# A fused attention and MLP kernel: dummy matmuls in longer pieces, and the list of steps in another order

## The chip, the cores and the metric

The kernel runs on one core of a Trainium2 chip. Its time is the device time of one execution in microseconds (us), taken as the median of several runs. The engines have their own instruction streams and run them strictly in order: TensorE (PE) for matrix products, VectorE (DVE) and ScalarE (ACT) for elementwise work, GpSimd (POOL) and SyncE (SP), which here mostly issue DMAs.

## The reference

Eight sequences ("images" in the step names, b = 0 to 7) with eight heads of 576 queries and 64 features. Each head has 16 beacon keys and values ahead of its own, and the mask is causal on the rest. The result, 4608 tokens of 512, goes through two matrix products with an ELU between them.

```python
scores = scale * np.matmul(q, k_all.transpose(0, 1, 3, 2))     # k_all = beacon_k, k
scores = np.where(causal, -1000000000.0, scores)
a = np.exp(scores - scores.max(-1, keepdims=True))
a /= a.sum(-1, keepdims=True) + 1e-09
x = np.matmul(a, v_all)        # v_all = beacon_v, v
...                            # heads side by side: x is 4608 x 512
h = x @ w_in                   # 512 x 2048
g = np.where(h > 0.0, h, np.exp(np.minimum(h, 0.0)) - 1.0)
return g @ w_out               # 2048 x 512
```

## The kernel before

The kernel is a set of small step functions and one long list of words. A word such as `F.3.10` calls the step `F` with the arguments 3 and 10. Every step issues its instructions in program order on the engines that it uses, so the list alone sets the order on each engine; across engines, semaphores hold an instruction until its operands are there and its buffer is free. There is no planner at run time: if an instruction has to wait, everything behind it on its engine waits too.

The steps that matter here:

- `warm.n` (L205) and `wm.n` (L212) are dummy matmuls on zeros, n of 512 columns or n of 128. They keep PE streaming in the opening, and nobody reads their result.
- `lq`, `lv`, `wi`, `wo` load queries and keys, values and weights. For images 0 to 2 `T` (L265) transposes queries and keys on PE, and `cq`, `ck` (L278) copy them out of PSUM on ACT or DVE.
- For images 3 to 7 `lk.b.0` and `lk.b.1` (L801) bring the queries and the keys of image b as bf16 into a scratch in device memory by POOL's queue; `lt.b.x` (L808) transposes one half of the heads of both out of that scratch, on SP's queue, into a buffer qst or kst (named by the half of the heads, two sets of buffers in turn); `lp.b.x` (L818) is a POOL copy of the beacon columns into the same buffer. The scores of a half need both loads and that half's own `lt` and `lp`.
- `S` (L319) are pieces of scores, `x` (L334) their exponentials on ACT, `m` (L339) the causal masks on DVE, `L` (L377) row sums, `W` (L377) the products with the values, `n` the reciprocal of the row sums by logarithm and exponential on ACT (L441, L444), `M` the scaling of the values' products on DVE.
- `F.t.i` (L518) is one piece of the first product for token tile t (512 tokens), `e` its exponential (L528), `u` its relu on ACT (L534) or, written `.v`, on DVE (L536), `k` (L548) the ELU put together on DVE. `r` and `g` (L555, L560) do the relu and the sum on DVE in another form, without `u`.
- `Q.t.a.b` (L625) are the matmuls a to b of the second product for tile t, in a scheme of seven half-size products instead of eight; `Z` builds sums of tiles for it on DVE (L573) or, written `.d`, by an accumulating DMA that POOL issues (L571). `J` (L642, L649) copies results out of PSUM and stores or accumulates them; some of those accumulations are POOL's (L656).
- For tiles 6 to 9 the first product is done by seven products too: `H`, `X`, `P` (L732), `K`, `E`, `U`, `V`.

POOL's DMAs take eight semaphore lanes in turn, DMASW0 to DMASW7: each of them waits for the landing of the one eight DMAs before it.

Of the kernel before, what the change touches and what calls it, by code (L numbers as in the profile page):

```python
# [17 lines left out]
def kernel(  # L18
# [819 lines left out]
    cq.0.3.1 S.0.3.1 m.0.3.0 x.0.3.1 m.0.0.3 L.0.A T.1.0.0 lv.0.0.1 m.0.2.2 n.0.A cq.1.0.0
    T.1.1.0 warm.4 S.0.2.1 ck.1.1.0 W.0.A.0 m.0.1.3 wi.2 S.0.3.3 W.0.A.1 x.0.2.1 M.0.A.0 M.0.A.1
    x.0.3.3 lv.0.3.4 S.1.1 S.0.3.2 cb.1.1 x.1.1 wi.1 x.0.3.2 m.0.2.3 m.0.3.3 F.0.4 cb.1.2 S.1.4  # L840
    m.0.3.2 x.1.4 e.0.4 L.0.B n.0.B W.0.B.0 S.1.3 x.1.3 F.0.3 r.0.4 g.0.4 cb.1.3 e.0.3 F.0.2
    M.0.B.0 S.1.0 u.0.2.v r.0.3 W.0.B.1 g.0.3 x.1.0 e.0.2 lq.1.0.4.8 T.1.2.0 M.0.B.1 F.0.5
    ck.1.2.0 u.0.5 T.1.3.0 k.0.2 S.1.6 m.1.0.0 F.1.5 e.0.5 cq.1.3.0 lq.2.0.0.4 x.1.6 S.1.2 H.1.1
    S.1.10 H.1.2 e.1.5 u.1.5.v k.0.5 F.1.2 u.1.2.v wi.0 x.1.10 F.1.4 x.1.2 e.1.2 k.1.5 S.1.5
    x.1.5 T.2.0.0 wi.3 u.1.4.v e.1.4 F.0.1 S.1.12 cq.2.0.0 F.0.0 u.0.1 T.2.1.0 x.1.12 e.0.1
    k.1.2 S.1.7 k.1.4 cq.2.1.0 e.0.0 F.1.0 x.1.7 S.1.11 u.0.0.v e.1.0 S.1.9 u.1.0.v lq.2.0.4.8
    F.0.6 x.1.11 S.1.8 x.1.9 k.1.0 x.1.8 F.1.6 u.0.6.v m.1.0.1 T.2.3.0 cb.2.3 e.0.6 T.2.2.0
    ck.2.3.0 m.1.1.1 ck.2.2.0 k.0.0 lv.1.0.1 m.1.1.0 F.0.7 cb.2.2 u.0.7.v lv.1.2.3.4 S.2.10
    x.2.10 wo.1 k.0.6 e.0.7 L.1.1 e.1.6 L.1.0 n.1.1 k.0.1 wo.0 n.1.0 u.1.6.v k.1.6 F.1.3 wo.2
# [136 lines left out]
```

## Time and profile before

| | before |
|---|---|
| median of 3 runs | 326.86 us (325.18 to 329.2) |
| the profiled execution's own time | 326.78 us |
| its span | 325.1 us |
| PE busy | 316.2 us (97%) |
| DVE busy | 294.0 us (90%) |
| ACT busy | 289.5 us (89%) |
| POOL busy | 122.0 us (38%) |
| granted PE clock, mean | 0.999 |

The span runs from the first busy instruction to the last; the 1.7 us between it and the execution's own time lie around it. Busy shares are means over the whole span, so the views by stretch of time, which the prediction shows, are needed beside them.

### The profile page before, as it was taken

The numbers are of one execution on the slowest core, as the hardware profiler recorded it, in microseconds if no ns is written. First come the engines' busy times: TensorE is split into PE (matmuls) and PEld (weight loads), VectorE is DVE, ScalarE is ACT, GpSimd is POOL, SyncE is SP. The second block draws the span as 40 slices with busy tenths as digits, with TensorE's granted clock in tenths as the row PEclk, the third lists the DMA queues.
The fourth block names the chain that finished last, engine by engine and source line by source line (L and its number), as shares of the span: only waits on it lengthen the run. The fifth ranks groups of instructions, "written<-read, shape, count | busy, mean of one in ns | idle before, by whom it ended". The sixth has DMA issues, their size and how long they took to land.

```text
span 325.1 us, 9115 instructions
## 1 busy us (share of the span) xinstructions
PE 316.2 (97%) x3743; PEld 226.4 (70%) x3744; DVE 294.0 (90%) x539; ACT 289.5 (89%) x479; POOL 122.0 (38%) x133
## 2 busy tenths in 40 slices
PE   8979999999999999999999999999999999999995
PEld 5647776656555655666555568788888888888884
DVE  2766998999989999989999999999999999998992
ACT  1988999998899999999999998999999999989910
POOL 8865693349318200527047085110401130041200
PEclk9999999999999999999999999999999999999999
DMA  9999999999999995599999997923293364476353
GB/s 112 167 183 202 190 193 183 155 156 168 158 172 165 187 103 105 78 175 149 175 141 153 179 78 104 124 68 98 35 162 67 66 96 68 100 87 123 89 93 129
DMA packets 141658, 42.53 MB, mean 131 GB/s; under 512 B 113201, under 2 KB 141617, under 8 KB 141617
## 3 DMA queue, kind: packets, MB, share of 16 engines
q0 software_dynamic: 106976, 26.35, 89.6%
q1 hardware_dynamic: 33920, 15.34, 23.4%
q8 instruction: 29, 0.48, 0.6%
q10 hardware_dynamic: 720, 0.26, 0.3%
q14 instruction: 13, 0.10, 0.1%
HBM read 37.22 MB, written 20.05 MB: 176 GB/s over the span
## 4 chain that ended last, share of the span: by engine, by line
PE 86%; ACT 6%; DVE 3%; DMA 2%; issue 1%; POOL 1%; DVEq 0%; POOLq 0%
PE ops L625 32%; PE hps L518 19%; PE hps L732 11%; PE sc L319 7%; PE ut L377 6%; PE sa L732 4%; ACT et L334 4%; PE sx L625 2%; PE lt L377 2%; DMA kst<-in_k_dram 2%; ACT e L528 1%; PE lt L426 1%; DVE hi L278 1%; ACT hi L278 1%; POOL qst L136 0%
## 5 line engine op out<-in xcount | busy, mean ns | idle before, releaser
L334 ACT ACTIVATE et<-sc 128x1024 f16<-128x1024 f32 (+2 forms) x114 | 104.8, 973 | 5.2 <-PE sc L319 5.0
L625 PEld LDWEIGHTS <-gt 128*128 128x128 f16 x864 | 83.2, 98 | 17.6 <-issue 1.2
L518 PE MATMUL hps<-xT,w_in 128*128 128x512 f16 (+1 forms) x384 | 79.7, 344 | 0.1
L656 POOL DMA_DIRECT2D out_dram<-osb x18 | 22.6, 1256 | 112.0 <-ACT osb L649 71.7
L625 PE MATMUL ops<-w_out,gt 128*128 128x256 f16 x416 | 55.0, 273 | 0.0
L625 PE MATMUL ops<-wt,gt 128*128 128x256 f16 x400 | 53.4, 273 | 0.0
L518 PEld LDWEIGHTS <-w_in 128*128 128x128 f16 x384 | 34.4, 98 | 27.0 <-issue 4.9
L548 DVE SCALAR_TENSOR_TENSOR gt<-e,r 128x512 f16<-128x512 f32 x74 | 49.5, 683 | 0.7 <-ACT r L534 0.4
L528 ACT ACTIVATE e<-hps 128x512 f32<-128x512 f32 x80 | 47.8, 617 | 2.4 <-PE hps L518 1.8
L149 POOL DMA_DIRECT2D v<-in_v_dram x40 | 38.2, 1226 | 17.2 <-issue 6.5
L777 DVE SCALAR_TENSOR_TENSOR gt<-e,r 128x512 f16<-128x512 f32 x64 | 42.7, 683 | 1.3 <-ACT e L760 0.5
L534 ACT ACTIVATE r<-hps 128x512 f16<-128x512 f32 x48 | 29.5, 622 | 0.3 <-DVE gt L548 0.3
L339 DVE TENSOR_TENSOR et<-et,triu 128x1024 f16<-128x1024 f16 (+5 forms) x66 | 27.0, 448 | 1.7 <-ACT et L334 1.7
L732 PEld LDWEIGHTS <-w_in 128*128 128x128 f16 x256 | 24.6, 98 | 4.2 <-issue 0.4
L760 ACT ACTIVATE e<-qst 128x512 f32<-128x512 f32 x40 | 25.8, 648 | 1.5 <-DVE qst L749 1.4
L573 DVE TENSOR_TENSOR gt<-gt 128x2048 f16<-128x2048 f16 (+1 forms) x24 | 25.8, 1083 | 0.0
L377 PEld LDWEIGHTS <-v 128*32 128x32 f16 (+1 forms) x800 | 17.4, 96 | 10.4 <-issue 3.0
L571 POOL DMA_DIRECT2D gt<-gt x6 | 9.7, 1619 | 35.8 <-DVE s L573 28.9
L749 DVE TENSOR_TENSOR qst<-hps,kst 128x512 f32<-128x512 f32 x32 | 21.5, 683 | 0.1
L536 DVE TENSOR_SCALAR r<-hps 128x512 f16<-128x512 f32 x26 | 17.9, 687 | 4.1 <-ACT e L528 2.7
L377 PE MATMUL ut<-et,v 128*32 128x464 f16 (+3 forms) x560 | 20.9, 296 | 0.0
L400 DVE TENSOR_TENSOR qkp<-qkp,et 128x1344 f16<-128x1344 f16 (+2 forms) x33 | 19.3, 585 | 0.5
(134 smaller groups left out, 561.8 us busy)
## 6 DMA issues: line engine op xcount, KB each, us to landing
out_dram<-sm SPq DMA_DIRECT2D x18, 256.0 KB, 2.4
out_dram<-osb POOLq DMA_DIRECT2D x18, 256.0 KB, 4.6
out_dram<-osb SPq DMA_DIRECT2D x17, 256.0 KB, 5.1
v<-in_v_dram POOLq DMA_DIRECT2D x24, 128.0 KB, 7.7
gt<-gt POOLq DMA_DIRECT2D x6, 512.0 KB, 7.1
scr<-in_q_dram POOLq DMA_DIRECT2D x5, 576.0 KB, 15.1
scr<-in_k_dram POOLq DMA_DIRECT2D x5, 576.0 KB, 16.2
w_in<-in_moe_w_in_dram POOLq DMA_DIRECT2D x8, 256.0 KB, 8.7
```

The lines of the kernel that those rows point to most:

```text
L149: nc.gpsimd.dma_start(out=vt[b][r0:r0 + n, j, :, :], in_=v[b, :, ilo[j]:ilo[j] + n, :].rearrange("h s d -> s h d"),)
L334: nc.scalar.activation(out=ets[b, d][:, :, a - EC2 * d:e - EC2 * d], in_=sc[b, g][:, :, a - c0:e - c0], func=AFT.Exp, bias=0.0, scale=SCALE)
L339: nc.vector.tensor_tensor(out=o, in0=o, in1=i, op=ALU.mult)
L377: nc.tensor.matmul(out=t[32 * i:32 * (i + 1), a - qa:e - qa], lhsT=ones[0:kc[j], :] if half is None else v16[0:kc[j], j, h, half:D:2], rhs ...
L518: nc.tensor.matmul(out=h[:, n_, :], lhsT=w_in16[:, cc, P * fc:P * (fc + 1)], rhs=xt[k][:, cc, a - TT * k:e - TT * k], start=(cc == 0), sto ...
L528: nc.scalar.activation(out=eb[t, i], in_=flat(hp[t, i]), func=AFT.Exp, bias=0.0, scale=1.0)
L534: nc.scalar.activation(out=rb[t, i], in_=flat(hp[t, i]), func=AFT.Relu, bias=0.0, scale=1.0)
L548: nc.vector.scalar_tensor_tensor(out=half(t, i), in0=eb[t, i], scalar=1.0, in1=rb[t, i], op0=ALU.subtract, op1=ALU.min)
L573: (nc.vector if eng == "v" else nc.gpsimd).tensor_tensor(out=o_, in0=a_, in1=b_, op=op_)
L625: nc.tensor.matmul(out=half_of(xy[t, n_], qd), lhsT=lw[:, P * qd:P * (qd + 1)], rhs=wt_[:, c, :], start=(first and c == 0 and (qd == 0 or ...
L732: nc.tensor.matmul(out=hx[t, g, n_][:, c, :], lhsT=lw, rhs=rh, start=(first and c == 0 and k_ == 0), stop=(k_ == 1), skip_group_check=True)
L777: eng.scalar_tensor_tensor(out=o_, in0=v_(eb[t, g, ph]), scalar=1.0, in1=v_(rb[t, g, ph]), op0=ALU.subtract, op1=ALU.min)
```

## The change

Only the list of words changes. In it, twelve `wm.4` (four dummy matmuls of 128 columns each) have become twelve `warm.1` (one of 512 columns). All other steps are there as before, with these exceptions in which engine does a piece: seven output copies net go from ACT to DVE, one copy of the first product's scheme and two relus of it from DVE to ACT, and among the plain relus three more are ACT's, two fewer DVE's, and one less takes the form `r`, `g`. The order of the words is another one from the first line on; in the opening PE's own order stays nearly what it was. The step functions are untouched, so their line numbers are the same in both.

The list has 1502 words in both; the first lines, and those around image 6's loads:

```diff
-    warm.4 wm.4 lq.0.0.0.4 wm.4 wm.4 wm.4 warm.4 lq.0.1.0.4 wm.4 ident bt bk wm.4 T.0.0.0 wm.4
-    cb.0.0 ck.0.0.0 cb.0.1 lq.0.0.4.8 T.0.1.0 S.0.0.0 T.0.0.1 cq.0.1.0 cq.0.0.1 S.0.1.0 x.0.0.0
...
+    warm.1 warm.1 warm.4 warm.1 warm.1 warm.1 warm.4 lq.0.0.0.4 lq.0.1.0.4 ident bt bk
+    lq.0.0.4.8 cb.0.3 T.0.0.0 warm.1 warm.1 cb.0.0 cb.0.1 ck.0.0.0 T.0.1.0 warm.1 lq.0.1.4.8
...
-    S.4.3 D.3.0.0 F.3.14 lk.6.1 Z.2.2.B m.3.0.1 m.3.1.0 D.3.0.1 Q.2.28.35 x.4.3 S.4.0 J.2.1
...
-    L.3.0 lk.6.0 u.3.10 Q.2.42.49 F.3.0 n.3.0 k.3.7 u.3.14.v e.3.14 Q.2.56.63 k.3.10 k.3.8 F.3.3
...
-    e.4.2 M.4.0.1 H.4.0 lp.6.0 S.5.7 u.4.2 S.5.2 x.5.7 F.4.8 Q.3.7.14 x.5.2 k.4.3 u.4.7.v S.5.11
-    S.4.12 F.4.9 J.2.6.v lv.5 H.4.1 e.4.8 Q.3.14.21 x.5.11 k.4.2 S.5.1 x.4.12 x.5.1 J.3.0.v
...
+    lk.6.0 M.4.0.0 u.4.7 e.4.11 e.4.7 J.2.5 k.4.7 Q.3.0.7 S.5.2 u.4.11.v x.5.2 Z.3.1.B.d S.5.7
...
+    Q.3.21.28 S.4.11 lk.6.1 x.4.11 J.3.0.v k.4.2 S.4.10 Z.3.2.B u.4.9.v k.4.9 Q.3.28.35 x.4.10
+    r.4.12 g.4.12 m.4.1.0 F.4.5 e.4.5 u.4.5 k.4.5 m.4.1.1 S.5.0 D.4.1.0 S.5.5 x.5.5 F.4.10 lv.5
+    F.4.1 J.3.1 Q.3.35.42 Q.3.42.49 lk.7.1 x.5.0 u.4.1.v e.4.10 S.5.9 D.4.1.1 S.5.10 e.4.1 x.5.9
+    Q.3.49.56 H.4.0 x.5.10 D.4.1.2 D.4.1.3 F.4.6 e.4.6 W.4.1 lt.6.0 u.4.10.v k.4.10 L.4.1 u.4.6
+    lp.6.1 k.4.1 J.3.2 m.5.1.0 F.4.15 F.4.14 Z.3.4.B n.4.1 lt.6.1 Q.3.56.63 m.5.0.1 e.4.15
+    lp.6.0 M.4.1.1 Q.3.63.70 M.4.1.0 u.4.15 u.4.14 F.4.0 J.3.3.v e.4.14 S.5.8 S.6.4 x.5.8 F.4.13
```

What this makes of the order on ACT in the opening, from the exponentials behind the first half's row sums of image 0 to the copy (L278) of image 1's transposed keys, e being an exponential of the first product and r its relu. Before:

```order
L441 ACTIVATE rl<-lt 128x640
L444 ACTIVATE rl<-rl 128x640
L334 ACTIVATE et<-sc 128x2x512
L528 ACTIVATE e<-hps 128x512
L334 ACTIVATE et<-sc 128x2x512
L528 ACTIVATE e<-hps 128x512
L278 COPY hi<-tp 128x2x576
L534 ACTIVATE r<-hps 128x512
```

And now:

```order
L441 ACTIVATE rl<-lt 128x640
L444 ACTIVATE rl<-rl 128x640
L334 ACTIVATE et<-sc 128x2x512
L528 ACTIVATE e<-hps 128x512
L334 ACTIVATE et<-sc 128x2x512
L528 ACTIVATE e<-hps 128x512
L534 ACTIVATE r<-hps 128x512
L278 COPY hi<-tp 128x2x576
L534 ACTIVATE r<-hps 128x512
```

One relu more stands ahead of the copy.

The other place is POOL's order around image 6 (buffers with their numbers: scr is the scratch, qst0 and kst0 the buffers of image 6, v16 the values of image 5, gt the tiles of the second product's third token tile, osb an output). Before, where the two loads of image 6 stand as the rows scr_2194 and scr_2305 some way ahead and the loads shown are those of image 7:

```order
L801 DMA scr_2194<-in_k_dram 4608x1x64
L818 COPY qst1_89<-bkT_111 128x2x16
L801 DMA scr_2305<-in_q_dram 4608x1x64
...
L818 COPY kst1_90<-bkT_111 128x2x16
L571 DMA gt_2083<-gt_2083 128x8x256
L818 COPY qst0_87<-bkT_111 128x2x16
L144 DMA v16_2812<-in_beacon_v_dram 16x8x64
...
L656 DMA out_0_dram<-osb_2896 128x2x256
L801 DMA scr_2959<-in_k_dram 4608x1x64
L801 DMA scr_2995<-in_q_dram 4608x1x64
L818 COPY kst0_88<-bkT_111 128x2x16
```

And now, where scr_2691 and scr_2826 are image 6's queries and keys, scr_2408 and scr_2912 those of image 7:

```order
L818 COPY kst1_90<-bkT_111 128x2x16
L801 DMA scr_2408<-in_q_dram 4608x1x64
L801 DMA scr_2691<-in_q_dram 4608x1x64
L571 DMA gt_2046<-gt_2046 128x8x256
L801 DMA scr_2826<-in_k_dram 4608x1x64
L144 DMA v16_2883<-in_beacon_v_dram 16x8x64
...
L656 DMA out_0_dram<-osb_2895 128x2x256
L801 DMA scr_2912<-in_k_dram 4608x1x64
L818 COPY kst0_88<-bkT_111 128x2x16
L818 COPY qst0_87<-bkT_111 128x2x16
```

The keys of image 6 have moved behind the accumulating DMA of the tile sum, and the copy into qst0 from ahead of image 5's values to behind the last load of image 7. By the lanes, scr_2912 waits for the landing of scr_2826, eight DMAs before it.

More of the change, by code (lines that the diff above doesn't have):

```diff
@@ L838 @@
[L838 to L849, printed above, removed]
@@ new lines @@
+    cq.1.0.0 S.0.3.1 m.0.0.3 ck.1.1.0 x.0.3.1 m.0.3.2 lv.0.0.1 cb.1.1 W.0.A.0 M.0.A.0 S.0.3.3
+    x.0.3.3 S.0.2.3 m.0.3.3 x.0.2.3 W.0.A.1 M.0.A.1 wi.2 S.1.1 S.0.2.1 m.0.2.3 x.1.1 x.0.2.1
+    m.0.2.2 F.0.4 m.0.0.2 S.1.4 lv.0.3.4 x.1.4 e.0.4 u.0.4.v L.0.B W.0.B.0 n.0.B S.1.3 wi.1
+    x.1.3 cb.1.3 F.0.2 e.0.2 M.0.B.0 r.0.2 g.0.2 F.0.3 S.1.0 x.1.0 e.0.3 u.0.3 W.0.B.1 M.0.B.1
+    lq.1.0.4.8 wi.0 T.1.2.0 F.0.5 ck.1.2.0 cb.1.2 lq.2.0.0.4 k.0.4 k.0.3 T.1.3.0 u.0.5 e.0.5
+    S.1.6 cq.1.3.0 F.1.5 m.1.0.0 x.1.6 e.1.5 u.1.5.v k.0.5 S.1.2 S.1.10 F.1.2 u.1.2.v F.1.4
@@ new lines @@
+    x.1.10 lv.1.0.1 S.1.5 x.1.2 T.2.0.0 u.1.4.v e.1.2 x.1.5 F.0.1 S.1.12 e.1.4 k.1.2 cq.2.0.0
+    k.1.4 u.0.1 x.1.12 wi.3 F.0.0 e.0.1 k.1.5 T.2.1.0 cq.2.1.0 S.1.7 F.1.0 e.0.0 x.1.7 e.1.0
+    u.0.0.v r.1.0 S.1.11 S.1.9 g.1.0 x.1.11 F.0.6 x.1.9 S.1.8 F.1.6 u.0.6.v x.1.8 lq.2.0.4.8
+    e.0.6 m.1.0.1 k.0.0 T.2.3.0 T.2.2.0 lv.1.2.3.4 u.1.6.v ck.2.3.0 cb.2.3 cb.2.1 F.0.7 ck.2.2.0
+    k.0.1 S.2.10 L.1.0 x.2.10 m.1.1.0 wo.2 wo.1 u.0.7.v m.1.1.1 cb.2.0 wo.0 k.0.6 e.1.6 L.1.1
+    e.0.7 k.0.7 F.1.3 k.1.6 n.1.0 M.1.0.0 lp.4.1 n.1.1 F.1.1 W.1.0 e.1.3 u.1.1 M.1.1.0 H.1.0
@@ new lines @@
+    M.1.0.1 W.1.1 M.1.1.1 S.2.4 e.1.1 u.1.3 k.1.1 x.2.4 F.1.7 u.1.7 k.1.3 F.2.8 S.2.3 wt.1.0
+    wo.3 e.1.7 k.1.7 e.2.8 S.2.1 Z.1.3.B u.2.8 F.2.13 Z.1.1.B x.2.3 F.2.7 x.2.1 S.2.2 lk.3.0
+    e.2.13 Q.1.0.7 H.1.2 lk.3.1 e.2.7 cb.2.2 x.2.2 lk.4.1 Q.1.7.14 wt.2.0 k.2.8 Q.1.14.21 u.2.7
+    S.2.6 lp.3.1 u.2.13 Z.1.2.B lv.3.0.1 x.2.6 S.2.5 J.1.0.v F.2.0 k.2.7 x.2.5 F.2.9 u.2.9
+    Q.1.21.28 wt.1.1 wt.2.1 Q.1.28.35 u.2.0 wt.4.1 S.2.11 lv.2.2.3.4 lv.2.0.1 e.2.9 k.2.9 lk.4.0
+    e.2.0 S.2.12 F.2.10 x.2.11 x.2.12 e.2.10 lt.3.1 k.2.0 F.2.5 lp.4.0 u.2.10 S.2.0 u.2.5.v
@@ new lines @@
+    S.2.8 Q.1.35.42 e.2.5 x.2.8 x.2.0 J.1.1 Q.1.42.49 J.1.2 F.2.3 k.2.5 F.2.6 S.2.9 m.2.0.1
+    e.2.6 k.2.10 u.2.6 wt.3.1 wt.3.0 S.2.7 Z.1.4.B lp.3.0 m.2.0.0 u.2.3 Q.1.49.56 k.2.6 e.2.3
+    D.2.0.0 k.2.3 D.2.0.1 D.2.0.2 D.2.0.3 x.2.9 Q.1.56.63 F.2.15 x.2.7 e.2.15 u.2.15 Q.1.63.70
+    F.2.12 J.1.3 e.2.12 Q.1.70.77 u.2.12 m.2.1.0 k.2.13 F.2.14 S.3.10 S.3.8 x.3.10 Q.1.77.84
+    x.3.8 k.2.15 u.2.14 e.2.14 F.2.1 L.2.0 lv.3.2.3.4 k.2.12 W.2.0 H.2.0 n.2.0 m.2.1.1 F.2.2
+    lt.3.0 lk.5.0 wt.4.0 Q.1.84.91 M.2.0.0 u.2.2 e.2.1 M.2.0.1 k.2.14 u.2.1 L.2.1 W.2.1 J.1.4
@@ new lines @@
+    n.2.1 F.2.11 e.2.2 M.2.1.1 M.2.1.0 F.2.4 u.2.11 S.3.7 lk.5.1 k.2.1 e.2.11 S.3.4 lt.4.0
+    lt.4.1 e.2.4 k.2.11 x.3.7 F.3.8 Q.1.91.98 Q.1.98.105 k.2.2 r.2.4 S.3.0 x.3.4 u.3.8.v g.2.4
+    S.3.2 Z.2.3.B x.3.0 x.3.2 e.3.8 J.1.5 H.1.1 Q.1.105.112 F.3.13 S.3.1 H.2.2 S.3.3 x.3.1
+    u.3.13.v Q.2.0.7 F.3.6 e.3.13 k.3.13 F.3.5 Z.2.1.B lp.5.0 x.3.3 S.3.6 u.3.6 J.1.6.v S.3.5
+    lt.5.0 m.3.0.0 e.3.6 k.3.8 u.3.5 Q.2.7.14 F.3.7 x.3.6 x.3.5 u.3.7.v k.3.6 Q.2.14.21 J.2.0.v
+    e.3.5 Z.2.2.B S.3.12 x.3.12 S.3.9 F.3.2 x.3.9 D.3.0.0 Q.2.21.28 Q.2.28.35 e.3.2 J.2.1 S.4.0
@@ new lines @@
+    lv.4 e.3.7 u.3.2 k.3.2 m.3.0.1 S.3.11 x.3.11 F.3.14 m.3.1.0 x.4.0 Q.2.35.42 F.3.3 S.4.3
+    u.3.14 S.4.5 D.3.0.1 D.3.0.2 D.3.0.3 Q.2.42.49 e.3.14 Q.2.49.56 x.4.3 S.4.4 k.3.5 k.3.7
+    x.4.5 W.3.0 Z.2.4.B H.4.2 x.4.4 e.3.3 J.2.2 k.3.14 L.3.0 n.3.0 Q.2.56.63 u.3.3.v F.3.0
+    F.3.10 m.3.1.1 e.3.0 M.3.0.0 Q.2.63.70 u.3.0 S.4.8 u.3.10 M.3.0.1 S.4.2 e.3.10 x.4.8 lt.5.1
+    F.3.9 D.3.1.0 Q.2.70.77 x.4.2 S.4.1 k.3.3 u.3.9.v e.3.9 S.4.6 F.3.1 lp.5.1 x.4.6 lk.7.0
+    D.3.1.1 k.3.9 D.3.1.2 x.4.1 D.3.1.3 J.2.3.v F.3.4 k.3.0 W.3.1 L.3.1 e.3.4 Q.2.77.84 u.3.1
@@ new lines @@
+    Q.3.14.21 S.5.1 x.4.12 S.5.6 e.4.2 F.4.12 x.5.6 H.4.1 x.5.1 F.4.9 k.4.8 e.4.9 e.4.12
+    Q.3.21.28 S.4.11 lk.6.1 x.4.11 J.3.0.v k.4.2 S.4.10 Z.3.2.B u.4.9.v k.4.9 Q.3.28.35 x.4.10
[3 more added lines that the diff above has]
+    lp.6.1 k.4.1 J.3.2 m.5.1.0 F.4.15 F.4.14 Z.3.4.B n.4.1 lt.6.1 Q.3.56.63 m.5.0.1 e.4.15
@@ new lines @@
+    k.5.13 F.5.15 u.5.12 F.5.10 Q.4.0.7 Q.4.7.14 x.6.0 x.6.6 e.5.10 u.5.15 D.5.1.1 S.6.9
+    Z.4.1.B.d lp.7.0 S.6.5 D.5.1.2 u.5.10.v F.5.0 e.5.15 D.5.1.3 lt.7.0 k.5.12 x.6.5 k.5.10
+    x.6.9 u.5.0 F.5.7 e.5.7 m.6.0.0 m.6.0.1 lt.7.1 L.5.1 e.5.0 u.5.7 D.6.0.0 n.5.1 k.5.7 k.5.0
+    W.5.1 Q.4.14.21 M.5.1.0 M.5.1.1 F.5.11 J.4.0 Z.4.2.B X.6.1 F.5.9 e.5.11 u.5.11 u.5.9 e.5.9
+    Q.4.21.28 S.7.0 S.6.8 F.5.1 F.5.4 k.5.11 H.1.3 x.6.8 Q.4.28.35 x.7.0 k.5.9 e.5.4 u.5.1
+    D.6.0.1 H.3.3 k.5.15 Q.4.35.42 D.6.0.2 e.5.1 u.5.4 k.5.1 S.6.12 x.6.12 J.4.1.v S.6.7 F.5.3
@@ new lines @@
+    x.6.7 X.6.3 F.5.5 Z.4.4.B S.6.11 S.6.10 D.6.0.3 Q.4.42.49 u.5.3 e.5.3 x.6.10 u.5.5 x.6.11
+    X.6.2 e.5.5 H.3.0 k.5.4 Q.4.56.63 F.5.8 u.5.8 e.5.8 H.3.2 L.6.0 J.4.2 W.6.0 H.2.3 P.6.0.0
+    k.5.3 K.6.0.0 n.6.0 k.5.5 X.6.4 P.6.0.1 Q.4.49.56 m.6.1.1 m.6.1.0 P.6.0.2 K.6.0.2 Q.4.63.70
+    K.6.0.1 P.6.0.3 k.5.8 M.6.0.0 J.4.3 Q.4.70.77 P.6.0.4 K.6.0.3 E.6.0.1 M.6.0.1 K.6.0.4
+    U.6.0.1 U.6.0.4 P.6.0.5 K.6.0.5 Q.4.77.84 Z.5.3.B P.6.0.6 Q.4.84.91 S.7.1 S.7.2 P.6.1.0
+    U.6.0.6 Z.5.1.B.d E.6.0.6 H.3.1 J.4.4 Q.4.91.98 x.7.1 E.6.0.4 K.6.1.0 H.4.3 P.6.1.1 D.6.1.0
@@ new lines @@
+    V.6.3.6 J.5.4 P.7.0.3 V.6.3.5 Z.6.3.B Z.6.1.B.d x.7.11 Q.5.91.98 P.7.0.4 K.7.0.3 Q.5.98.105
+    Q.5.105.112 U.7.0.1 X.7.4 J.5.5 K.7.0.4 E.7.0.1 P.7.0.5 E.7.0.4 m.7.0.1 P.7.0.6 E.7.0.6
+    Q.6.0.7 K.7.0.5 P.7.1.0 V.7.0.1 U.7.0.6 U.7.0.5.v Q.6.7.14 U.7.0.4 P.7.1.1 K.7.1.0 J.5.6
+    E.7.0.5 D.7.0.1 P.7.1.2 K.7.1.2 V.7.0.4 Q.6.14.21 K.7.1.1 P.7.1.3 S.7.8 D.7.0.2 U.7.1.1
+    K.7.1.3 V.7.0.5 S.7.7 x.7.8 D.7.0.3 P.7.1.4 V.7.0.6 K.7.1.4 P.7.1.5 m.7.1.1 x.7.7 m.7.1.0
+    E.7.1.1 Q.6.21.28 P.7.1.6 K.7.1.5 V.7.1.1 E.7.1.6 J.6.0 W.7.0 U.7.1.6 L.7.0 P.7.2.0 Z.6.2.B
@@ new lines @@
+    U.7.1.4 P.7.2.1 E.7.1.4 V.7.1.6 Q.6.28.35 Q.6.35.42 K.7.2.0 K.7.2.1 D.7.1.0 U.7.1.5 D.7.1.1
+    J.6.1 E.7.1.5 P.7.2.2 K.7.2.2 V.7.1.5 P.7.2.3 Q.6.42.49 P.7.2.4 K.7.2.3 P.7.2.5 J.6.2
+    K.7.2.4 Q.6.49.56 E.7.2.1 U.7.2.1 P.7.2.6 V.7.1.4 Q.6.56.63 V.7.2.1 E.7.2.4 K.7.2.5
+    Q.6.63.70 D.7.1.2 U.7.2.6 P.7.3.0 U.7.2.4 V.7.2.4 D.7.1.3 E.7.2.6 J.6.3 K.7.3.0 Z.6.4.B
+    P.7.3.1 n.7.0 Q.6.70.77 K.7.3.1 P.7.3.2 K.7.3.2 Q.6.77.84 M.7.0.0 U.7.2.5.v P.7.3.3 E.7.2.5
+    P.7.3.4 M.7.0.1 W.7.1 K.7.3.3 U.7.3.1 L.7.1 P.7.3.5 Q.6.84.91 E.7.3.1 J.6.4 Q.6.91.98
@@ new lines @@
+    K.8.1.4 V.8.0.6 E.8.1.1 K.8.2.0 V.8.1.1 P.8.2.2 P.8.1.6 U.8.1.4 K.8.2.3 K.8.2.2 J.7.0
+    E.8.1.4 E.8.1.5 Z.7.1.B.d U.8.1.5.v Z.7.2.B P.8.2.1 E.8.1.6 P.8.2.5 K.8.2.5 U.8.1.6 P.8.2.4
+    Q.7.28.35 Q.7.35.42 V.8.1.4 J.7.1 K.8.2.4 Q.7.42.49 U.8.2.1 P.8.2.6 E.8.2.4 V.8.1.5 P.8.3.3
+    V.8.1.6 P.8.3.0 U.8.2.5 E.8.2.1 Q.7.49.56 Q.7.56.63 K.8.3.0 E.8.2.6 P.8.3.2 U.8.2.6 J.7.2
+    Z.7.4.B P.8.3.1 K.8.3.2 V.8.2.1 K.8.3.3.v X.9.1 V.8.2.6 X.9.2 E.8.2.5 Q.7.63.70 U.8.2.4.v
+    U.8.3.1 V.8.2.5 P.8.3.4 X.9.3 E.8.3.1 J.7.3 K.8.3.4 P.9.0.0 K.9.0.0 P.8.3.5 K.8.3.5
@@ new lines @@
+    J.8.0 V.9.1.1 V.9.0.4 E.9.1.4 Z.8.2.B P.9.2.1 Q.8.21.28 E.9.1.5 U.9.1.6 E.9.1.6 V.9.1.6
+    K.9.2.3 U.9.1.4 P.9.2.2 K.9.2.2 Q.8.28.35 V.9.1.4 P.9.2.5 J.8.1 U.9.2.1 P.9.3.0 U.9.1.5.v
+    E.9.2.1 P.9.2.4 K.9.2.5 Q.8.35.42 P.9.3.3 K.9.2.4 V.9.2.1 Z.8.4.B E.9.2.5 K.9.3.0 V.9.1.5
+    P.9.2.6 K.9.3.3 U.9.2.5 Q.8.42.49 P.9.3.2 U.9.2.6 Q.8.49.56 K.9.3.2 U.9.2.4.v V.9.2.5
+    E.9.2.4 V.9.2.4 P.9.3.1 J.8.2.v P.9.3.4 P.9.3.5 E.9.2.6 Q.8.56.63 Q.8.63.70 K.9.3.4 E.9.3.4
+    U.9.3.4.v V.9.3.4 P.9.3.6 J.8.3 E.9.3.6 V.9.2.6 U.9.3.1 U.9.3.6 Q.8.70.77 K.9.3.5 U.9.3.5
@@ L957 @@
+    Q.8.77.84 J.8.4.v E.9.3.1 E.9.3.5 V.9.3.6 V.9.3.1 Q.8.84.91 V.9.3.5 Q.8.91.98 Q.8.98.105
+    J.8.5 Z.9.3.0 Q.9.0.7 Z.9.1.0 Z.9.3.1 Z.9.1.1 Q.9.7.14 Z.9.2.0 Q.8.105.112 Q.9.14.21 Z.9.2.1
+    Q.9.21.28 J.9.0 Q.9.28.35 J.9.1 Q.9.35.42 Q.9.42.49 J.9.2.v Q.9.56.63 Q.9.63.70 Q.9.49.56
+    Z.9.4.1 Z.9.4.0 Q.9.70.77 J.8.6.v J.9.3.v Q.9.77.84 Q.9.84.91 J.9.4 Q.9.91.98 Q.9.98.104
+    Jh.9.0 J.9.5 Q.9.104.112 Jh.9.1
     """)
```

146 lines of the change are left out of this document (39 added, 107 removed).

## The prediction

> **What bounds the kernel now.** I read the head of the page first, then the busy time of each engine by stretch, then TensorE's (PE's) waits, then the timelines of the places where it waits. The head:
>
> ```profile
> span 325.1 us, 9115 instructions
> PE 316.2 (97%) x3743; PEld 226.4 (70%) x3744; DVE 294.0 (90%) x539; ACT 289.5 (89%) x479; POOL 122.0 (38%) x133
> ...
> PEclk9999999999999999999999999999999999999999
> ```
>
> PE is busy for 97% of the span and its clock is granted in full in every slice. The profiled execution's own time is 326.78 us, 1.7 above its span, and it lies next to the median of the runs, 326.86; all sums below start from 326.78. The stretches (columns: length, then busy time of PE, weight loads, DVE, ACT, POOL):
>
> ```profile
> 0.00:8.00 8.00, 6.74 (x46) 4.34 (x47) 2.10 (x10) 1.29 (x2) 6.77 (x15) 1.00 0.91 111
> 8.00:52.00 44.00, 40.15 (x817) 28.66 (x817) 34.94 (x83) 40.71 (x56) 32.48 (x42) 1.00 1.48 188
> 52.00:300.00 248.00, 247.82 (x2689) 174.47 (x2687) 238.78 (x418) 238.29 (x405) 80.43 (x75) 1.00 1.16 124
> 300.00:326.00 26.00, 21.50 (x197) 18.96 (x195) 18.19 (x32) 9.16 (x19) 2.35 (x2) 0.97 0.44 101
> ```
>
> From 52 to 300 us PE is idle for 0.18 of 248 us. Whatever holds PE up there lengthens the kernel one for one, and no other order of the same matmuls can be quicker there. Only the opening, 8 to 52, has something to win: 3.85 us of PE idle, with ACT (40.71) as busy as PE (40.15). Of that idle time one wait has no visible cause:
>
> ```profile
> PE ua L377 <- issue: 1.3, 1, 1.3
> ```
>
> **The dummies.** Twelve groups of four 128-column matmuls (L212) become twelve of one with 512 (L205): the columns streamed are the same, 36 matmuls and 36 weight loads go.
>
> ```profile
> 1.26 1.89 PE L205 MATMUL w<-lo 128*128 128x512 bf16 x4 [1.26 <-DVE lo L172]
> 2.94 1.91 PE L212 MATMUL w<-lo 128*128 128x128 bf16 x16
> 4.65 1.91 PE L205 MATMUL w<-lo 128*128 128x512 bf16 x4
> 6.36 0.63 PE L212 MATMUL w<-lo 128*128 128x128 bf16 x4
> ...
> 7.21 0.40 PE L212 MATMUL w<-lo 128*128 128x128 bf16 x4
> 7.54 0.30 PE L265 MATMUL tq<-late,qst 128*64 128x128 bf16 x4
> ...
> 13.73 0.62 PE L212 MATMUL w<-lo 128*128 128x128 bf16 x8
> 14.29 0.35 PE L319 MATMUL sc<-qkp 64*128 64x128 bf16 x6
> ```
>
> Starts against next starts: at the beginning four of 512 take 1.68 us (1.26 to 2.94) and sixteen of 128 take 1.71 (2.94 to 4.65), so one long costs 0.42 and four short 0.43: equal. Later four short take 0.33 with what surrounds them (7.21 to 7.54) or 0.28 in a row of eight (0.56, 13.73 to 14.29), and a long one 0.25 (three from 20.36 to 21.10 below). Seven groups stand in that later part, so the saving is 7 x 0.03 to 7 x 0.08, 0.2 to 0.6 us of PE time; all of it lies where ACT leads, so I let 0 to −0.2 of it reach the end. I take **−0.05**.
>
> **The invisible wait.** It stands in the middle of one row of 24 value matmuls that need nothing new:
>
> ```profile
> 20.36 0.81 PE L205 MATMUL w<-lo 128*128 128x512 bf16 x3 [0.16 <-issue]
> 21.10 0.35 PE L319 MATMUL sc<-hi 64*128 64x320 bf16 x4
> ...
> 22.16 0.55 PE L377 MATMUL ua<-et,v 128*32 128x256 f16 x18
> 23.97 0.25 PE L377 MATMUL ua<-et,v 128*32 128x144 f16 x6 [1.26 <-issue]
> ```
>
> and the DMA view of 21 to 24.5 us shows one packet of instructions just there:
>
> ```profile
> q8 instruction: 1, 0.02, 1.7%
> ```
>
> So PE ran out of instructions (an inference: time and queue agree, nothing else is missing). ACT pays for it:
>
> ```profile
> 21.51 1.63 ACT L334 ACTIVATE et<-sc 128x832 f16<-128x832 f32 x2
> 24.59 2.75 ACT L334 ACTIVATE et<-sc 128x1024 f16<-128x1024 f32 x3 [1.45 <-PE sc L319]
> ```
>
> ACT was through at 23.14 and its next scores came at 24.59. Without the wait they would have come at 23.33, so the wait is worth at most 1.26. With 36 instruction pairs less and other words around it, the same count of PE instructions falls in another, slower stretch (row sums of 40 matmuls in a row, with PE's queue fuller), where the packet may come in time; the next packet may then be the late one. Ends: −1.26 (gone) and +1.26 (gone there, a second and third one later; or kept and one more). I take **−0.6**, half of what it costs, since nothing in the rows says that packets are late elsewhere: this is the only such wait over 0.2 us. The Trainium skill, "Runtime: NRT & Kernel Launch", section "Instruction fetch mechanics", says that instructions come in blocks of 16 KiB, 256 of them, fetched ahead, and that crossing a boundary is "mostly hidden". By that the term would be 0; the row above, with 1.26 us in the open, disagrees for this one boundary.
>
> **ACT in the opening.** The order of ACT before and after differs by one relu between 30 and 35 us: an ELU whose relu DVE computed before (or DVE did whole) now has it on ACT, ahead of the copy of image 1's transposed keys.
>
> ```profile
> L534 ACT ACTIVATE r<-hps 128x512 f16<-128x512 f32 x2 | 1.2, 610 | 0.0
> ```
>
> One of them is 0.61 us. ACT leads in this stretch (3.29 us idle in 44, of which 1.45 is the wait above), so it reaches the end unless ACT's remaining idle takes it: 0 to +0.61, and up to +1.2 if the scores behind it slip a bank as well. I take **+0.6**.
>
> **The rest of the order.** Net, seven output copies go from ACT to DVE, and a few ELU pieces back:
>
> ```profile
> L642 ACT COPY sm<-ops 128x512 f32<-128x512 f32 x23 | 14.0, 609 | 0.4 <-PE ops L625 0.3
> L649 DVE COPY osb<-ops 128x512 f32<-128x512 f32 x3 | 2.0, 682 | 0.0
> ```
>
> ACT −7 x 0.61 plus one copy (0.61) and five relus (0.62 to 0.65), about −0.5; DVE +7 x 0.68 less the pieces that leave, about +1.4. DVE has 9.2 us idle between 52 and 300, so the cover holds: **0**. Were DVE late in some place, the price would be one of its pieces, 0.68, times the few places. The number of matmuls of each kind is the same, and so are PE's switches between kinds, within one or two; the end keeps the same last five steps.
>
> **Image 6's keys and queries.** This is the one edit that can cost something on PE. The load of image 6's keys into the scratch (POOL, L801) used to be issued some twenty steps ahead; now it stands behind the accumulating DMA of a tile sum (L571), and after it POOL takes six value loads, one output, and image 7's keys, whose issue waits for the semaphore lane of image 6's keys, then the two copies of beacon columns (L818). The rows of before:
>
> ```profile
> 133.34 1.56 POOL L571 DMA_DIRECT2D gt<-gt  x1 [25.46 <-DVE s L573]
> 134.25 0.93 POOL L818 COPY qst<-bkT 128x32 bf16<-128x32 bf16 x1
> ...
> 148.69 2.72 POOL L801 DMA_DIRECT2D scr<-in_k_dram  x1
> ...
> 152.12 1.94 POOL L818 COPY kst<-bkT 128x32 bf16<-128x32 bf16 x1
> ```
>
> ```profile
> 156.47 0.39 PE L319 MATMUL sc<-kst 64*128 64x272 bf16 x4
> 156.80 0.39 PE L319 MATMUL sc<-qst 64*128 64x192 bf16 x4
> ```
>
> The scores of image 6 begin at 156.8 (the first that read qst). In the new order two F pieces (0.95 each: 1.90 for two at 153.87) stand ahead of them that stood behind, and one Q piece of seven matmuls (0.8) the other way: 156.8 + 1.9 − 0.8 = 157.9. The tile sum that POOL waits for has three more Q pieces, an F piece, three of scores and the row sums and values of image 4's first half ahead of it, some 5.5 us of PE's work: it comes at 138.8 if it keeps step with PE, at 133.3 if DVE is through as early as now. Its issue takes 1.56, so image 6's keys are issued between 134.9 and 140.4; I take 138.8, in the upper half, since DVE's own pieces ahead of it moved along with PE's. Their landing, and the transposes behind them (SP, L808):
>
> ```profile
> L801 POOL DMA_DIRECT2D scr<-in_k_dram x1: 2720/2720/2720, 148.7 to 148.7; - x1
> ...
> DMA to landing us min/median/max: 10.4/12.7/15.1
> ```
>
> ```profile
> DMA to landing us min/median/max: 10.4/15.1/21.3
> ```
>
> ```profile
> L808 SPq DMA_TRANSPOSE qst<-scr x2: 1927/2910/3893, 141.4 to 143.5; - x2
> ...
> DMA to landing us min/median/max: 6.0/6.5/7.0
> ```
>
> The first is the two such loads from 135 to 155 us, the second all ten, the third the transposes of image 6. Behind the landing the transposes (6.0 to 7.0) and, side by side, POOL's image 7 issue (2.72), and two copies (2.2 and 0.93, together 5.9) are needed. So image 6 is ready 6.5 after the landing: at 138.8 + 10.4 + 6.5 = 155.7, + 12.7: 158.0, + 15.1: 160.4, with ends of 154 and 161 or so; against 157.9 that is a stall of 0, 0.1, 2.5, ends 0 and 3.2. I take **+0.5**, nearer to the middle one, since those loads ran at the same hour of the kernel. Waiting there is PE, and behind it everything.
>
> **Sum.** 326.78 − 0.05 − 0.6 + 0.6 + 0 + 0.5 = **327.2**. At the low ends (−0.2, −1.26, 0, 0) 325.3, and the runs' own spread below the median (1.7) leaves 323.6 (325.3 − 1.7); at the high ends (0, +1.26, +1.2, +3.2) 332.4. The range goes from 323.6, and to take in rival B below from **322.7**, to **332.4**. A change counts as faster below 320.3 and slower above 333.4, 2% either way, which is about what the spread of the runs (325.18 to 329.2) lets one tell.
>
> **Rivals.**
> A. PE waits for image 6 in earnest, slower: if the load lands as late as the latest of ten, 21.3, the scores come at 138.8 + 21.3 + 6.5 = 166.6, 8.7 behind 157.9, and nothing makes that good in a stretch with 0.18 us idle: 326.78 + 8.7 = 335.5, some **335**. It decides from a landing of 19.2 (stall 6.6) on. For it: right behind the load six value loads enter the same queue, which holds 89.6% of sixteen engines' span. Against: the two loads of that hour took 10.4 and 15.1.
> B. The new opening feeds ACT well enough that PE's idle there vanishes: 326.78 − 3.85 = **322.9**. For it: fewer steps stand between scores and exponentials near the invisible wait. Against: ACT is busy 40.71 of 44 itself and gets one relu more.
> C. The clock stays at half for longer, because the dummies stand elsewhere between the transposes. The row of L205, durations min, median and max in ns:
>
> ```profile
> L205 PE MATMUL w<-lo x11: 379/634/634, 1.3 to 20.8; 128*128 128x512 bf16 x11
> ```
>
> 634 against 379 shows two speeds; by the starts above, the slow one lasts from 1.26 to about 6.8, 5.5 us. A second such stretch does 2.75 us of work in 5.5: 326.78 + 2.8 = **329.6**. Against: the same thirteen times 512 columns stand ahead of the first transpose in both. "TensorE: Matmul & The Clock Gate", Part 1, in the Trainium skill has a gate that opens after a busy window of about 3.4 us that runs free of the kernel's start, and its Part 4 has transposes not count as busy; the first agrees with a slow stretch of one to two windows, the second no run here shows.
>
> **Chances.** Forecast 0.70 (0.68 within 2%, 0.02 slower), A 0.16 (slower), B 0.07 and C 0.05 (both within 2%), a gain of over 2% 0.02, which would need more than all idle time of the opening. Together: faster 0.02, within 2% 0.80, slower 0.18. Outside the range lie A and the gain of over 2%, 0.18.
>
> **What would show it.** Right: PE busy 247 to 248 of 52:300; no wait of PE's on L377 by issue near 24 us, or one at a row of L377 a little later; dummies L205 x24 (x23 if a record is missing again) and no L212; image 6's keys landing 10 to 15 us after an issue at 137 to 140, and a PE wait of 0 to 3 us at scores that read qst near 158. Wrong: a PE wait over 4 us anywhere after 52, PE's busy time in 8:52 up by more than 2, or slow matmuls after 9 us.

## The result and the profile after

The changed kernel takes **339.8 us** (median of 4 runs, 337.2 to 342.1) against 326.2 for the one before (4 runs). The ratio is 1.041, 95% interval 1.035 to 1.046: slower by 4%. The forecast was 327.2, with a range up to 332.4.

The head of the page of the changed kernel, whose profiled execution took 342.08 us:

```profile
span 340.4 us, 9035 instructions
PE 320.5 (94%) x3705; PEld 225.8 (66%) x3708; DVE 296.8 (87%) x540; ACT 289.4 (85%) x478; POOL 126.2 (37%) x133
...
PEclk9679999999999999999999859999999999999999
```

DVE and ACT have about as much to do as before (294.0 and 289.5); the span grew by waiting, and in two places the clock (PEclk) is down, with which PE's busy time rises too (316.2 before). The busy time by stretch says where (columns as before, the last three being the granted clock, the share of the DMA engines and GB/s):

```profile
8.00:52.00 44.00, 40.30 (x734) 27.84 (x740) 32.20 (x72) 39.87 (x53) 26.23 (x38) 0.88 1.42 180
52.00:300.00 248.00, 237.52 (x2619) 163.64 (x2609) 230.21 (x407) 225.73 (x380) 85.78 (x77) 0.98 1.21 119
```

From 52 to 300 us PE is idle for 10.5 us where it was 0.18. PE's waits name the owner:

```profile
PE ops L625 <- DVE gt L573: 8.0, 1, 8.0
PE sc L319 <- DVE gt L548: 1.9, 1, 1.9
```

One single wait of 8.0 us, at the second product of tile 4, and one of 1.9. PE's timeline at the first, and DVE's row that it waits for:

```profile
189.95 0.60 PE L625 MATMUL ops<-w_out,gt 128*128 128x256 f16 x4
198.59 1.68 PE L625 MATMUL ops<-wt,gt 128*128 128x256 f16 x7 [8.03 <-DVE gt L573]
```

```profile
197.30 1.23 DVE L573 TENSOR_TENSOR gt<-gt 128x2048 f16<-128x2048 f16 x1 [9.81 <-DMA gt<-gt]
```

So DVE in turn waits 9.8 us for a DMA, gt<-gt, which it wanted at 197.30 − 9.81 = 187.5: the accumulating DMA of a tile sum, `Z.4.1.B.d`. The prediction looked at its sister of tile 3 and passed this one over. POOL's timeline, which issues it, and SP's beside it:

```profile
172.30 1.20 POOL L656 DMA_DIRECT2D out_dram<-osb  x1 [16.54 <-ACT et L334]
173.06 1.00 POOL L144 DMA_DIRECT2D v<-in_beacon_v_dram  x1
173.61 4.67 POOL L149 DMA_DIRECT2D v<-in_v_dram  x5
177.77 1.73 POOL L656 DMA_DIRECT2D out_dram<-osb  x1
179.17 1.93 POOL L571 DMA_DIRECT2D gt<-gt  x1
```

```profile
173.82 5.78 SPq L808 DMA_TRANSPOSE qst<-scr  x2
179.70 10.03 SPq L808 DMA_TRANSPOSE kst<-scr  x2
```

```profile
DMA to landing us min/median/max: 18.0/18.0/18.0
```

The last line is that of L571 between 165 and 185 us. The same of the kernel before, with SP's timeline there and DVE's use of the sum:

```profile
L571 POOL DMA_DIRECT2D gt<-gt x1: 1568/1568/1568, 168.5 to 168.5; - x1
...
DMA to landing us min/median/max: 6.9/6.9/6.9
```

```profile
165.61 3.99 SPq L808 DMA_TRANSPOSE qst<-scr  x2
178.24 0.37 SPq L654 DMA_DIRECT2D out_dram<-osb  x1
178.70 4.68 SPq L808 DMA_TRANSPOSE kst<-scr  x2
```

```profile
184.17 1.21 DVE L573 TENSOR_TENSOR gt<-gt 128x2048 f16<-128x2048 f16 x1
```

Before, the sum was issued at 168.5, between the two pairs of image 7's transposes, landed at 175.4 and was wanted at 184.2: 8.8 us to spare. Now it is issued 10.6 later, takes 11.1 longer, and is wanted at 187.5, 3.3 later: 10.6 + 11.1 − 8.8 − 3.3 = 9.6, about the 9.8 that DVE waits.

The two stretches at half clock, one in the opening of this execution and one behind the wait, the latter from where PE starts again:

```profile
11.45:21.68 10.23, 8.82 (x140) 5.38 (x140) 5.47 (x20) 8.57 (x11) 8.38 (x13) 0.52 1.60 171
```

```profile
198.60:202.60 4.00, 4.00 (x22) 2.11 (x23) 4.00 (x10) 3.04 (x6) 0.00 (x0) 0.50 0.00 0
```

The 4.0 us at half clock behind the wait cost half their length, 2.0. The span grew by 15.3: 8.0 and 2.0 for the sum, 1.9 for image 6, some 0.6 in smaller waits after 52 us, and what is left, 2.8, I put to the opening's half-speed stretch. That stretch comes and goes between executions of one order: the other three executions of the change had mean clocks of 0.984 to 0.989, against 0.969 here, which leaves room for about one stretch of 10 us at half clock (it takes 0.015 off the mean) in place of two.

### The profile page after: what moved, and what is told of

The parts are those of the page before. It is cut to its first block, busy times and chain, and to the rows that moved or that the text cites. A ratio compares the mean times of both kernels' runs of the same rounds, so it can differ in the third digit from the quotient of the medians.

```text
span 340.4 us, 9035 instructions
## 1 busy us (share of the span) xinstructions
PE 320.5 (94%) x3705; PEld 225.8 (66%) x3708; DVE 296.8 (87%) x540; ACT 289.4 (85%) x478; POOL 126.2 (37%) x133
## 4 chain that ended last, share of the span: by engine, by line
PE 34%; DVE 19%; DMA 8%; ACT 6%; issue 2%; DVEq 0%; ACTq 0%
PE ops L625 16%; PE hps L732 9%; DMA gt<-gt 8%; DVE gt L548 4%; DVE qkp L400 4%; DVE gt L573 2%; PE sx L625 2%; DVE et L339 2%; ACT e L760 2%; PE sa L732 2%; PE hps L518 2%; DVE xT L478 2%; PE ut L377 2%; PE sc L319 2%; ACT r L767 1%
## 5 line engine op out<-in xcount | busy, mean ns | idle before, releaser
L656 POOL DMA_DIRECT2D out_dram<-osb x18 | 24.1, 1341 | 110.2 <-ACT osb L649 61.9
L528 ACT ACTIVATE e<-hps 128x512 f32<-128x512 f32 x80 | 48.9, 634 | 10.9 <-DVE gt L548 9.5
L534 ACT ACTIVATE r<-hps 128x512 f16<-128x512 f32 x51 | 31.2, 632 | 1.9 <-PE hps L518 1.9
L571 POOL DMA_DIRECT2D gt<-gt x6 | 9.8, 1630 | 49.8 <-DVE s L573 48.1
L377 PEld LDWEIGHTS <-v 128*32 128x32 f16 (+1 forms) x800 | 17.5, 96 | 9.5 <-issue 1.7
L377 PE MATMUL ut<-et,v 128*32 128x464 f16 (+3 forms) x560 | 20.9, 296 | 0.0
L536 DVE TENSOR_SCALAR r<-hps 128x512 f16<-128x512 f32 x24 | 16.4, 686 | 4.4 <-ACT e L528 3.5
```

Of the source, the lines that this page charges most:

```text
L377: nc.tensor.matmul(out=t[32 * i:32 * (i + 1), a - qa:e - qa], lhsT=ones[0:kc[j], :] if half is None else v16[0:kc[j], j, h, half:D:2], rhs ...
L528: nc.scalar.activation(out=eb[t, i], in_=flat(hp[t, i]), func=AFT.Exp, bias=0.0, scale=1.0)
```

## The experiments

All of them move words of the list or leave words out, except where `.d` or `wm` is said. Each ran beside the kernel before on its chip, whose median was 325.8 to 326.1.

**The sum of tile 4, three ways.** Theory Q: it is late since it queues behind POOL's value loads. Rival X: the transposes on SP's queue hold its packets. Rival N: something else would have cost the same.

```diff
 # values later
-x.6.1 F.5.2 lv.6 e.5.2 x.6.3
+x.6.1 F.5.2 e.5.2 x.6.3
...
-lt.7.1 L.5.1
+lt.7.1 lv.6 L.5.1
```

> The new order, with image 6's value loads (lv.6) moved from ahead of the accumulating DMA of tile 4's sum (Z.4.1.B.d) to behind the last transposes of image 7. Theory Q (the sum's DMA lands late because it is issued behind six value loads on POOL and its packets queue behind theirs): it is issued about 5 us earlier and lands within 7 to 10 us, PE's wait of 8.0 us at tile 4's second product and the half-speed stretch behind it go, the time is 329 to 331. Rival X (it is the transposes of image 7 on SP's queue that hold its packets): it still takes 13 us or more to land, PE waits 2 us or more, 332 to 336. Rival N (the wait only shows what some later thing would cost anyway): 338 to 341.

Measured: 331.3 us (ratio 1.013, 1.005 to 1.021). The sum is issued at 171.2, eight us earlier (it is wanted 3.7 earlier, at 183.8), and still takes 14.1 to land:

```profile
L571 POOL DMA_DIRECT2D gt<-gt x1: 2527/2527/2527, 171.2 to 171.2; - x1
...
DMA to landing us min/median/max: 14.1/14.1/14.1
```

DVE waits 1.5 us for it, and PE's 8.0 us are gone; after 52 us image 6's wait (1.7) and 0.7 us at another place are left. The time lies 0.3 above what Q gave, the landing is what X gave: what saved it was more the earlier issue than the quicker transfer (14.1 for 18.0).

```diff
 # no transposes of image 7
-S.6.5 D.5.1.2 u.5.10.v F.5.0 e.5.15 D.5.1.3 lt.7.0 k.5.12 ... m.6.0.1 lt.7.1 L.5.1
+S.6.5 D.5.1.2 u.5.10.v F.5.0 e.5.15 D.5.1.3 k.5.12 ... m.6.0.1 L.5.1
```

> The new order without the transposing loads of image 7 (lt.7.0 and lt.7.1 left out, so image 7 is scored against stale keys). Theory Q: the sum's DMA of tile 4 still takes 13 to 18 us to land behind the value loads, PE still waits 4 to 8 us, 335 to 340. Rival X: it lands in 7 to 10 us, PE's wait goes, 329 to 331. If both queues share the blame, the landing is between, 10 to 13 us, and the time 331 to 335.

Measured: 329.1 (1.008, 1.003 to 1.013). The value loads still stand ahead of the sum, and it lands in 8.4:

```profile
L571 POOL DMA_DIRECT2D gt<-gt x1: 2602/2602/2602, 176.1 to 176.1; - x1
...
DMA to landing us min/median/max: 8.4/8.4/8.4
```

So most of the long landing comes from the transposes, as X said. Behind six value loads alone the sum is all but in time: DVE waits 0.5 us, PE not at all. By what means the transposes hold it up, no run here separates. In the kernel before, two of them, issued 2.9 and 0.6 us ahead of the sum and landed by 172.5, left it at 6.9.

```diff
 # sum on DVE
-Z.4.1.B.d
+Z.4.1.B
```

> The new order with tile 4's sum made by DVE (Z.4.1.B) in place of the accumulating DMA. Theories Q and X alike: PE's wait of 8.0 us and the half-speed stretch go, DVE has 1.2 us more, so 329 to 331. Rival N: 338 to 341.

Measured: 329.3 (1.009, 1.006 to 1.013). PE's longest wait after 52 us is image 6's, and the clock is full from 150 to 200 us:

```profile
PE sc L319 <- DVE gt L548: 1.1, 1, 1.1
```

```profile
150.00:200.00 50.00, 48.73 (x545) 29.90 (x543) 48.89 (x91) 46.38 (x78) 11.78 (x13) 1.00 1.26 122
```

So N falls: by the medians this one DMA was worth 10.5 of the 13.6 us.

**The one move in the old order.** If the late sum is the cause, the kernel before must lose by that move alone.

```diff
-Z.4.3.B F.5.2 Z.4.1.B.d lp.7.0 e.5.2
+Z.4.3.B F.5.2 lp.7.0 e.5.2
...
-D.5.1.2 lv.6 D.5.1.3
+D.5.1.2 lv.6 Z.4.1.B.d D.5.1.3
```

> The old order with the accumulating DMA of tile 4's sum (Z.4.1.B.d) moved behind image 6's value loads (lv.6), as the new order has it: that one move alone, with the two transposes of image 7's second half right behind it and those of its first half long done. DVE wants the sum at 184.2. It is issued at some 177.5. If the move alone makes the loss: it lands 10 us or more later, 187.5 or later, PE waits 3 us or more, 329 to 335. If the loss needs all four transposes of image 7 beside it (theory X): it lands in 7 to 9 us, 184.5 to 186.5, PE waits 0 to 2 us, 325.5 to 328.

Measured: 333.6 (1.022, 1.017 to 1.028). PE's waits and the landing:

```profile
PE ops L625 <- DVE gt L573: 4.8, 1, 4.8
```

```profile
L571 POOL DMA_DIRECT2D gt<-gt x1: 2097/2097/2097, 177.5 to 177.5; - x1
...
DMA to landing us min/median/max: 11.8/11.8/11.8
```

Two transposes issued at 178.9 and 180.8 are enough for 11.8 behind the value loads, so the move alone makes a loss of 2%; with four of them it is 14 to 18.6. The loss is 7.8 us by the medians for 4.8 us of wait. Behind the wait PE runs at half clock from 190.7 to 195.8, which is some 2.6 us more; this execution has a stretch at half clock in its opening too, of 3.4 us.

**The dummies.** Length alone, in both orders.

```diff
 # the new order
-warm.1
+wm.4        # at each of the 12 places
```

> The new order with each of the twelve warm.1 replaced by wm.4 at its place: the length of the dummies alone undone. Theory P (in the opening the half-speed stretch comes from where the dummies stand, not from their length): as the change, 338 to 341. Rival D (four short matmuls keep the clock where one long does not): the opening's half-speed stretch goes, 2.6 us less, 336 to 338.

Measured: 335.6 (1.028, 1.023 to 1.034). The wait for the sum is there with 3.9 us, no half-speed stretch in the opening of the profiled execution, and an issue wait of 0.8 us at L377 that the change does not have. Neither theory gave 335.6. By the traces the wait for the sum is 4.1 shorter and image 6's wait of 1.9 is gone, which is more than the 4.2 us between the medians; the clock in the opening is not needed for them.

```diff
 # the old order
-wm.4
+warm.1      # at each of the 12 places
```

> The old order with each wm.4 replaced by warm.1 at its place: the length of the dummies alone. Theory P: as before, 325.5 to 327. Rival D: a half-speed stretch in the opening, 328 to 330.

Measured: 325.3 (0.998, 0.994 to 1.001), and, again with more rounds:

> The old order with warm.1 at the place of each wm.4, again, in more rounds. Theory I (36 instruction pairs less move PE's instruction packet to where it is hidden; the invisible wait at L377 goes): 0.5 to 1.2 us below the old kernel, ratio 0.996 to 0.999, interval clear of 1. Rival: ratio 1 within 0.002.

325.5 (1.000, 0.996 to 1.004). The dummies' length is worth nothing that can be measured. The issue wait, 1.26 us in the kernel before, is in neither of their traces; it is in all four others that keep the short dummies, with 0.8, 0.7, 0.7 and 0.6 us. That it goes is shown; that it saves time is not.

**The opening.** Each opening with the other's rest.

```diff
 # new opening: the new list up to and with F.0.5, then the old list's other words
 # old opening: the old list up to and with F.0.5, then the new list's other words
```

> The new order up to F.0.5 (some 31 us), then all other words in the old order. If the new opening costs what the aligned traces show (2.8 us by 52 us, most of it the half-speed stretch): 328 to 330. If it costs nothing: 325.5 to 327.

Measured: 325.7 (0.999, 0.997 to 1.001): the new opening costs nothing, one relu more on ACT or not.

> The old order up to F.0.5, then all other words in the new order. The waits for image 6 and for tile 4's sum stay: 336 to 338, with PE waiting some 8 us for the sum; if the new opening costs nothing, 339 to 341.

Measured: 334.7 (1.025, 1.020 to 1.030), with 6.0 us of PE wait for the sum. The loss is in the rest of the list. It is some 2 us less than expected, as the wait is 6.0 for 8.0. Image 6's wait, expected to stay, is gone, as with the short dummies: its keys landed no earlier (after 15.9 and 15.4 us, 15.4 in the change), but the transposing load behind them landed after 6.7 and 7.0 us, where the change took 9.6. Why waits at 160 and 190 us shrink when the first 31 us run otherwise is not settled.

**Image 6.** Its keys moved back in the new order, then that with the sum on DVE, and the reverse move in the old order.

```diff
 # keys of image 6 early, in the new order
-M.4.0.1 lk.6.0 M.4.0.0
+M.4.0.1 lk.6.0 lk.6.1 M.4.0.0
...
-Q.3.21.28 S.4.11 lk.6.1 x.4.11
+Q.3.21.28 S.4.11 x.4.11
```

> The new order with image 6's key load (lk.6.1) moved back right behind image 6's query load (lk.6.0), ahead of the accumulating sum of tile 3. Theory K (the two waits are one chain: keys 6 late, so keys 7 late by the lane, so the transposes of image 7 late, so they meet tile 4's sum): PE's wait for image 6 (1.9 us) goes, the transposes of image 7 begin before 170 us, the sum lands within 10 us, 328 to 331. Rival S (two separate faults; the transposes of image 7 are held on SP's queue by the output stores ahead of them): only image 6's 1.9 us go, the sum still takes 14 us or more, 336 to 338.

Measured: 332.9 (1.022, 1.017 to 1.026). The wait for image 6 is gone, but the sum still lands late, so rival S holds: two faults, not one chain. The transposes of image 7 begin at 170.85, still right behind an output store on SP at 170.37, and meet the sum:

```profile
L571 POOL DMA_DIRECT2D gt<-gt x1: 2771/2771/2771, 172.0 to 172.0; - x1
...
DMA to landing us min/median/max: 18.6/18.6/18.6
```

```profile
PE sc L319 <- issue: 2.6, 1, 2.6
PE ut L377 <- issue: 1.8, 1, 1.8
PE ops L625 <- DVE gt L573: 1.7, 1, 1.7
```

The first row is marked as issue, but it ends at 187.36, some 0.1 us after the second of image 7's transposes landed (issued at 172.5, 14.8 to landing): it is image 7's scores that wait. The 2.6 us (and the 1.8 at 53 us, one more of the instruction waits) have made PE late, so only 1.7 are left for the sum, and the time came out below the expected 336 to 338.

> The kernel with the sum of tile 4 on DVE, and image 6's key load moved back as well. If the rest of the loss after the sum is image 6's wait (1.1 to 1.9 us): 326 to 328, and no PE wait over 0.6 us after 52 us. If something else holds it: 329, as with the sum on DVE alone.

Measured: 327.8 (1.005, 1.002 to 1.008), 1.5 below the kernel with the sum on DVE alone (on another chip), as image 6's wait there, 1.1 us, would have it; no PE wait above 0.54 is left after 52 us. Of the last 2 us against the kernel before, 1.35 are four waits of 0.2 to 0.54; the rest, and with it what the pieces that changed engines cost, is open.

```diff
 # keys of image 6 late, in the old order
-F.3.14 lk.6.1 Z.2.2.B
+F.3.14 Z.2.2.B
...
-Z.3.1.B.d S.5.3
+Z.3.1.B.d lk.6.1 S.5.3
```

> The old order with image 6's key load moved behind the accumulating sum of tile 3 (Z.3.1.B.d), as the new order has it: that one move alone. Keys issued at some 134.5, landed 10 to 15.5 us later at 145 to 150, second transpose landed 7 to 9.6 us behind that, 152 to 160; scores of image 6 wanted at 156.8: PE wait 0 to 3 us, 326 to 329. Theory K adds nothing here, as the keys of image 7 do not wait in their lane for long.

Measured: 326.0 (1.001, 0.997 to 1.004), no wait: the keys landed after 11.3 us and image 6's scores ran at 155.75. Alone, the move of the keys is harmless; in the new order the same load took 15.4 and the transposing load behind it 9.6 (8.9 here).

No version beats both kernels by an amount that can be told: the two best, 325.3 to 325.7, are within 0.2% of the kernel before.

## Why the prediction was wrong

- **What bounds the kernel: right.** A wait of PE after 52 us costs its length; it cost more, 2.0 us on top, by the clock behind it.
- **"The rest of the order": the step that failed.** It was put at 0 after looking at the balance of DVE and ACT, and image 6's loads were called "the one edit that can cost something on PE". In its place stand some 10.5 us: the sum of tile 4, an accumulating DMA like the one of tile 3 that was traced, moved behind six value loads and an output on POOL, and into the transposes of image 7, so that it was issued at 179.2, landed after 18.0 in place of 6.9, and made PE wait 8.0. The rows for it stood in the trace of before: the issue at 168.5, the second pair of transposes from 178.7 on, the use at 184.2. The slack of 8.8 us was not worked out, nor was it asked whether the landing of 6.9 us would hold beside other transfers. The prediction's own sign of being wrong, a PE wait of over 4 us after 52, came with 8.0.
- **Image 6: right in kind, too small.** Forecast: keys issued at 138.8, landed after 10.4 to 15.1, transposes 6.5, a stall of 0.5, at most 3.2. Measured:

```profile
161.97 0.40 PE L319 MATMUL sc<-qst 64*128 64x192 bf16 x4 [1.92 <-DVE gt L548]
```

  The view names DVE, which had long been done: the second transpose was issued at 152.3, when the keys had landed (136.9 + 15.4), and landed at 161.9, 9.6 later instead of 6.5. PE, ready for the scores at 160.0, waited 1.9. Both transfers ran slower than their rows of before; that more transfers ran beside them is the likely reason, but no run separates it. The upper end of 3.2 was added up too low: the latest issue and landing, 140.4 + 15.1 + 6.5, make a stall of 4.1.
- **The dummies (−0.05): right**, nothing either way. **The invisible wait (−0.6):** it is gone as forecast, but no time could be shown for it. The waits of all kernels with short dummies fall at about the same 350th matmul, and the one of 1.8 us in the new order with image 6's keys early at about the 862nd, four times 128 further. The Trainium skill, "Runtime: NRT & Kernel Launch", "Instruction fetch mechanics", has instructions fetched in blocks of 256, which are 128 matmuls with their weight loads; the places agree with it, while its "mostly hidden" does not fit the 0.6 to 1.8 us. That PE waits there for instructions stays an inference from place and count.
- **ACT's relu (+0.6): wrong**, the new opening costs nothing that can be measured (ratio 0.999, 0.997 to 1.001).
- **Rival A** had the right sign and by luck nearly the size of the wait (8.7 us of PE for 8.0), but the wrong DMA. **Rival C** did appear in the profile, but also in two profiled executions of the old order, one with short dummies and one with long. The dummies' length does not make it more frequent there: a mean clock of 0.990 or less (these two have 0.985 and 0.979), in executions 2 to 4 us longer than the median, is on record for 5 of 22 with long dummies and for 15 of 73 of the kernel before (one of 401 us left out), and for none of 10 with the new opening. **Rival B** fell: the new opening with the old rest gained nothing.
- **The chances:** slower had 0.18. The mistake was to price one moved load with care and to leave the accumulating sums, six in the kernel, at nothing in a list that was reordered from end to end.

## What to carry to other kernels

When an order changes as a whole, go through every DMA that somebody waits for: when it lands, when it is wanted, how far each moves. The smallest slack, not the most conspicuous move, decides. A transfer's landing time holds only for its neighbours in time, so ask which transfers of other queues it will now run beside. A longer wait on PE is dearer than its length: behind all four waits of 3.9 us or more (3.9, 4.8, 6.0 and 8.0) PE ran at half clock for 3.4 to 5.1 us, behind those of 2.6 us and less at the full clock.
